# Retention and a cosine-gated MLP on one core: q is loaded four tokens to a partition, and x leaves PSUM in steps

## The chip, the cores and the metric

The kernel runs on one core of a Trainium2 chip. The metric is the device time of one execution in microseconds. Before the change it was 308.84 us, the median of three runs (305.84 to 311.0). The engines are called by the names of the profile: PE is the matrix engine (PEld its weight loads), DVE the vector engine, ACT the scalar engine, POOL GpSimd, and SP the engine that here only issues DMAs. A name with a q behind it (SPq, ACTq) is that engine's instruction queue, where DMAs are issued.

## The reference

```python
# q, k, v: (8 batches, 8 heads, 576 tokens, 64); w_in (512, 2048); w_out (2048, 512); all float32
scores = (1 / 8) * q @ k.T                       # per batch and head
Dmat   = where(i >= j, gamma[h] ** (i - j), 0)   # gamma[h] = 1 - 2 ** (-5 - h)
attn   = (scores * Dmat) @ v
x = attn.transpose(0, 2, 1, 3).reshape(4608, 512)
h = x @ w_in
out = (h * cos(h)) @ w_out                       # (4608, 512) float32
```

The decay factors into a number per query row and one per key row: gamma^(i-j) = gamma^i * gamma^(-j). So q is multiplied by gamma^i / 8 and v by gamma^(-j), a causal mask of zeros and ones is left, and what lies in earlier blocks of the sequence can be carried along as a state of 64 x 64 numbers per head.

## The kernel before

**Retention.** A batch of 576 tokens is cut into five blocks (`NCH`), four of 128 tokens and a last one of 64 (`ck_of`; `ns_of` is 2 for the long blocks and 1 for the short one). The eight heads of a block are worked on together. A block passes through these steps:

1. `load` brings k, q and v of the block from HBM in float32, each by two DMAs on SP's queue. One DMA takes four heads (`half(hs)`: heads 0 to 3 into partitions 0 to 63, heads 4 to 7 into partitions 64 to 127). A partition holds two neighbouring tokens of each of its four heads, so a row of a transfer is 2 x 64 floats, 512 bytes, in the long blocks, and 256 bytes in the short one.
2. `kcast` turns k into bfloat16, and `decay` multiplies q by the table UQ and v by the table WV, both into bfloat16. k and q land side by side in the tile KQ. These three run on POOL in most blocks, on DVE in some of the first ones.
3. k and q are transposed, so that the 64 numbers of a head lie along partitions (tile KQT). For batches 0 and 1 `turn` does that on PE, with a copy by ACT; from batch 2 on `prep_dma` has SP issue one DMA transpose per block.
4. `scores` multiplies k and q by PE, for each of the two token places of a partition and for head pairs, into the PSUM banks SC; DVE multiplies by the mask MK and leaves the tile RT.
5. `rest` adds up, in the PSUM tile PS, the part from the state and the part from RT and v, and in further columns of PS the block's share of the next state. ACT then copies the result into the bfloat16 tile XT, which holds x transposed: features along partitions, tokens along columns. Columns of PS stand in the order of the token's place in its partition first (64 tokens of place 0, then 64 of place 1); the copy reads them straight and writes every second column, so that XT is in the tokens' order. `state` adds the block's share to the running state.

The tables UQ and WV are made in `consts` at the start: POOL writes token numbers into IP (`iota`), DVE corrects them for the upper 64 partitions, and ACT takes sixteen small exponentials, one per head and table.

**The MLP.** x is worked on in nine tiles of 512 tokens. `mlp1` multiplies XT by w_in for one of sixteen groups of 128 hidden features, ACT takes the cosine, and DVE multiplies. The second product is done for the first tile by `mlp2` in the plain way, and for the others by `layer2`, with seven products of quarter size and sums of quarters in place of eight products.

**The order.** Everything is written out by hand in `emit`, and each engine runs its own instructions in that order, held back only by semaphores. PE has two things to do in turn: the MLP of tile j, and in between the blocks of batch j + 1. Within `layer2` of tile j the five blocks of batch j + 1 are visited at steps 0, 3, 6, 9 and 12 (`VISITS`: `rest` of the block before, `scores` of this one). `prep_dma` of blocks 0 and 1 of batch j + 2 stands in `layer2` of tile j (`PREP2`), that of blocks 2 to 4 in `mlp1` of tile j + 1 (`PREP1`).

**SP's queue.** At the start SP issues k, q and v of the five blocks of batch 0, in that order. After that `loads_to` keeps the loads three blocks ahead of the preparation (`LEAD`). Each of the fifteen staging tiles (k, q, v for five blocks) exists once, so a load waits until the cast or decay of the batch before has read its tile. From batch 2 on SP issues for each block a transpose, which waits for that block's three POOL instructions, and then the six loads of a later block. The stores of the result go out on ACT's queue, but for the last ones. The weights are loaded by POOL's queue in eight transfers, which cast to bfloat16, in the first 50 us.

The change touches `load`, `decay`, `scores`, `rest` and `consts`.

Of the kernel before, what the change touches and what calls it, by code (L numbers as in the profile page):

```python
# [6 lines left out]
ALU = mybir.AluOpType  # L7
# [7 lines left out]
NP = H_ // 2  # L15
# [28 lines left out]
def ns_of(r):  # L44

    return ck_of(r) // 64


# [92 lines left out]
class _Kernel:  # L141
    def __init__(self, nc, es, q, k, v, w_in, w_out, out):
# [52 lines left out]
        self.bOSB = [Buf() for _ in range(4)]  # L195
        self.IP = sb("ip", [128, NIP], F32)
        self.WV = sb("wv", [128, NIP * 4], F32)
        self.UQ = sb("uq", [128, NIP * 4], F32)
# [6 lines left out]
        self.C_PIH = sb("c_pih", [128, 1], F32)  # L205
        self.bIP, self.bWV, self.bUQ, self.bMK, self.bC, self.bID, self.bIDLE = (Buf() for _ in range(7))

# [19 lines left out]
    def consts(self):  # L227
        s = self.s
        s.op("dve", lambda e: e.memset(self.C_LN8.ap(), float(math.log(1.0 / 8.0))), writes=[Buf()])
        s.op("dve", lambda e: e.memset(self.C_PIH.ap(), float(math.pi / 2.0)), writes=[self.bC])  # L230
        s.op("dve", lambda e: e.memset(self.IDLE.ap(), 0.0), writes=[self.bIDLE])
        self.touch(AF.Exp)

        for t, b, o, n, pat, base, mul in (
                (self.IP, self.bIP, 0, NIP, [[CH, NCH - 1], [1, 2]], 0, 2),
                (self.IP, self.bIP, NIP - 1, NIP, [[0, 1]], CH * (NCH - 1), 1),
                (self.MI, self.bMK, 0, 2 * CH, [[-1, 2], [1, 2], [2, 64]], 0, -2)):
            shape = [[n, 128]] + [[1, 1]] if o else [[n, 128], [1, n - 1]] if n == NIP else [[n, 128], [128, 2], [64, 2], [1, 64]]
            s.op("pool", lambda e: e.iota(bass.AP(t, o, shape), pat, base=base, channel_multiplier=mul,
                                          allow_small_or_imprecise_dtypes=True), writes=[b])  # L240
        for o, n in ((0, NIP - 1), (NIP - 1, 1)):
            up = bass.AP(self.IP, 64 * NIP + o, [[NIP, 64], [1, n]])
            s.op("dve", lambda e: e.tensor_scalar(up, up, -128.0 if n > 1 else -64.0, None, ALU.add),
                 reads=[self.bIP], writes=[self.bIP])
# [12 lines left out]
        for t, b, sign in ((self.UQ, self.bUQ, 1.0), (self.WV, self.bWV, -1.0)):  # L257
            for h in range(H_):
                hs, hh = divmod(h, 4)
                s.op("act", lambda e: e.activation(  # L260
                    bass.AP(t, 64 * hs * 4 * NIP + hh, [[4 * NIP, 64], [4, NIP]]),
                    bass.AP(self.IP, 64 * hs * NIP, [[NIP, 64], [1, NIP]]), AF.Exp, scale=sign * self.lng[h],
                    **(dict(bias=bass.AP(self.C_LN8, 64 * hs, [[1, 64], [1, 1]])) if sign > 0 else {})),
                    reads=[self.bIP, self.bC], writes=[Buf()])
            b.w = [Tok("act", "act", s.count["act"], {})]

# [6 lines left out]
    def load(self, x, b, r, after=()):  # L273
        ns = ns_of(r)
        t, bt = self.ST32[x][r], self.bST32[x][r]

        def half(hs):
            dst = bass.AP(t, 64 * hs * 256 * ns, [[256 * ns, 64], [D_ * ns, 4], [1, D_ * ns]])
# [3 lines left out]

        return self.s.dma("sp", f"{x}n{r}", [half(0), half(1)], writes=[bt], after=after)

# [26 lines left out]
    def decay(self, eng, x, b, r):  # L311
        ns, i = ns_of(r), b % 2
        if x == "q":
            o, bt, w, bw = self.by_head(self.KQ[i][r], 256 * ns, 512 * ns, ns, D_, 256), self.bQB[i][r], self.UQ, self.bUQ
        else:
            o, bt, w, bw = self.by_head(self.VB[i][r], 0, 256 * ns, ns, D_ * ns, D_), self.bVB[i][r], self.WV, self.bWV
        self.s.op(eng, lambda e: e.tensor_tensor(  # L317
            o, self.by_head(self.ST32[x][r], 0, 256 * ns, ns, D_ * ns, D_),
            bass.AP(w, r * 8, [[4 * NIP, 128], [1, 4], [4, ns], [0, D_]]), ALU.mult),
            reads=[self.bST32[x][r], bw], writes=[bt])  # L320

# [50 lines left out]
    def scores(self, b, r):  # L372
# [3 lines left out]
        for c in range(2):  # L376
            for sl in range(ns):
                for hs in range(2):
                    for hp in range(2):
# [3 lines left out]
                            bass.AP(self.KQT[i], k0 + sl * 256, [[W, 64], [1, 64]]),  # L383
                            bass.AP(self.KQT[i], k0 + 256 * ns, [[W, 64], [256, ns], [1, 64]]),
                            dict(start=c == 0 and sl == 0, stop=c == 1 and sl == ns - 1, skip_group_check=True)))
        self.group(mms, [self.bKT[i][r], self.bQT[i][r]], self.bSC)
        for hp in range(2):
            p3 = [[512, 128], [ns * nq, 2], [1, ns * nq]]
            s.op("dve", lambda e: e.tensor_tensor(  # L389
                bass.AP(self.RT[r % 2][hp], 0, p3), bass.AP(self.SC[hp], 0, p3),  # L390
                bass.AP(self.MK, 0, [[2 * CH, 128], [0, 2], [1, ns * nq]]), ALU.mult),
                reads=[self.bSC[hp], self.bMK], writes=[self.bRT[r % 2][hp]])

    def rest(self, b, r, state=True):
# [39 lines left out]
        n0 = min(ck, XR - t0)  # L434
        for x0, po0, n in ((t0, 0, n0), (0, n0 // ns, ck - n0)):
# [412 lines left out]
```

## Time and profile before

| | |
|---|---|
| time, median of 3 runs (range) | 308.84 us (305.84 to 311.0) |
| time of the profiled execution, and its span | 309.18 us, 307.1 us |
| mean granted clock of PE over the span | 0.989 |
| matmuls | 3520, busy 292.3 us |
| loads of q: transfers, size | 64 of 128 KB and 16 of 64 KB |
| q, from issue to landing (median) | 3.4 us (128 KB), 3.0 us (64 KB) |
| SP's time to issue a load of q (least, median, most) | 595, 617, 2167 ns |
| SP's time to issue a transpose (least, median, most) | 1227, 1282, 2208 ns |
| POOL's decay of q, long block (mean) | 1101 ns |
| ACT's copy of x out of PSUM (mean) | 748 ns long, 392 ns short block |
| ACT's copy of a transpose out of PSUM, 128x512 (mean) | 595 ns |
| HBM read, written | 36.70 MB, 9.44 MB |

The span is the time from the first to the last instruction of the program on the core; the time of an execution has some two microseconds more around it. In the profile's groups, a line reads: line of the source, engine, operation, tile written <- tiles read, size, count, then the busy time in us, the mean of one instruction in ns, and the idle time of the engine ahead of them with what ended it. The page cuts the span into 40 slices of 7.7 us and gives each engine's busy share in tenths; the row DMA is the mean busy share of the 16 DMA engines. A line of a DMA queue gives packets, megabytes, and the time the packets took as a share of 16 engines over the span. The chain of waits is followed back from the last instruction, and gives what each stretch of the time was spent on.

### The profile page before, as it was taken

To read this page: it belongs to the slowest core of one execution; us is meant where nothing else is said; L and a number is where in the kernel's file an instruction comes from. 1 tells how busy PE (TensorE), PEld (TensorE's weight loads), DVE (VectorE), ACT (ScalarE), POOL (GpSimd) and SP (SyncE) were. 2 spreads that over 40 slices of the span, in tenths; PEclk is the share of its full clock that TensorE was granted. 3 is DMA by queue.
4 is the path that set the end of the run, shared out by engine and by line. 5 is a ranking of instruction groups with operands and counts; after the bars stand their busy time and mean duration, and the time that the engine had idled before them with its cause. 6 is when DMAs were issued, how large, how long until landed. Compare 5 with 4: busy or idle time off the path is not lost.

```text
span 307.1 us, 8716 instructions
## 1 busy us (share of the span) xinstructions
PE 292.3 (95%) x3520; PEld 190.6 (62%) x3520; DVE 232.3 (76%) x393; ACT 190.1 (62%) x336; POOL 115.8 (38%) x133
## 2 busy tenths in 40 slices
PE   8768997999899999999999999999999999999996
PEld 3347644553587458746874687457845874685485
DVE  3347654867986898789878986999689768937963
ACT  6647845587565766576657665865576657724730
POOL 2346271999835444533551445436341000000000
PEclk9969999999999999999999999999999999999999
DMA  4999999567986987697879799977795012003003
GB/s 137 204 203 218 215 235 235 156 162 198 235 177 184 280 129 189 169 269 161 164 180 260 160 174 170 290 168 173 191 254 97 2 50 89 2 0 130 10 0 140
DMA packets 103480, 49.60 MB, mean 162 GB/s; under 512 B 45456, under 2 KB 98960, under 8 KB 103440
## 3 DMA queue, kind: packets, MB, share of 16 engines
q1 hardware_dynamic: 94176, 35.80, 54.2%
q10 hardware_dynamic: 5040, 9.05, 8.8%
q0 software_dynamic: 4224, 4.19, 8.4%
q8 instruction: 28, 0.46, 0.6%
q14 instruction: 12, 0.10, 0.1%
HBM read 36.70 MB, written 9.44 MB: 150 GB/s over the span
## 4 chain that ended last, share of the span: by engine, by line
PE 82%; DVE 5%; ACT 4%; SPq 4%; DMA 2%; issue 1%; POOL 0%; DVEq 0%; ACTq 0%
PE mm L362 59%; PE mm L364 14%; PE ps L362 6%; SPq L281 4%; PE sc L362 3%; DMA kn<-in_k_dram 2%; ACT cb L482 2%; DVE gt L485 1%; DVE ss L542 1%; DVE rt L389 1%; ACT sb L456 1%; ACT xt L439 1%; ACT kqt L348 1%; DVE ss L485 1%; DVE s L453 0%
## 5 line engine op out<-in xcount | busy, mean ns | idle before, releaser
L362 PE MATMUL mm<-xt,win 128*128 128x512 bf16 (+5 forms) x517 | 119.0, 349 | 2.0 <-DVE gt L485 1.2
L482 ACT ACTIVATE cb<-mm,c_pih 128x512 bf16<-128x512 f32 (+3 forms) x147 | 98.7, 680 | 33.7 <-PE mm L364 30.0
L485 DVE TENSOR_TENSOR gt<-mm,cb 128x512 bf16<-128x512 f32 (+1 forms) x130 | 85.7, 678 | 11.8 <-ACT cb L482 8.2
L362 PEld LDWEIGHTS mm<-xt,win 128*128 128x128 bf16 x517 | 46.8, 99 | 49.5 <-ACT cb L482 4.0
L364 PE MATMUL mm<-xt,win 128*128 128x512 bf16 (+5 forms) x147 | 54.0, 368 | 0.0
L389 DVE TENSOR_TENSOR rt<-sc,mk 128x512 bf16<-128x512 f32 (+1 forms) x80 | 44.8, 601 | 11.4 <-PE sc L364 11.4
L308 POOL CAST kq<-kn 128x512 bf16<-128x512 f32 (+1 forms) x40 | 25.2, 629 | 66.3 <-DMA kn<-in_k_dram 66.3
L317 POOL TENSOR_TENSOR kq<-qn,uq 128x512 bf16<-128x512 f32 (+1 forms) x37 | 36.9, 997 | 20.8 <-DMA qn<-in_q_dram 19.1
L362 PE MATMUL mm<-tt,ss 128*128 128x256 bf16 x336 | 43.2, 273 | 0.0
L439 ACT ACTIVATE xt<-ps 128x512 bf16<-128x512 f32 (+1 forms) x41 | 27.0, 661 | 24.6 <-PE ps L364 18.6
L317 POOL TENSOR_TENSOR vb<-vn,wv 128x512 bf16<-128x512 f32 (+1 forms) x34 | 34.4, 1013 | 17.1 <-DMA vn<-in_v_dram 14.4
L456 ACT ACTIVATE sb<-s 64x256 bf16<-64x256 f32 x64 | 26.6, 416 | 13.3 <-DVE s L453 12.1
L362 PEld LDWEIGHTS mm<-tt,ss 128*128 128x128 bf16 x336 | 31.4, 98 | 4.8
L566 ACT ACTIVATE sn<-mm 128x512 f32<-128x512 f32 x31 | 18.5, 598 | 25.1 <-PE mm L364 24.8
L542 DVE TENSOR_TENSOR ss<-gt 128x512 bf16<-128x512 bf16 (+1 forms) x56 | 32.1, 573 | 0.9
L571 DVE TENSOR_TENSOR osb<-mm,sn 128x512 f32<-128x512 f32 x30 | 20.6, 687 | 11.6 <-PE mm L364 11.3
L362 PE MATMUL mm<-wout,gt 128*128 128x256 bf16 x217 | 28.0, 273 | 0.3 <-DVE gt L485 0.3
L362 PE MATMUL mm<-wout,ss 128*128 128x256 bf16 (+1 forms) x160 | 27.4, 305 | 0.0
L453 DVE TENSOR_TENSOR s<-ps,s 128x256 f32<-128x256 f32 x24 | 10.2, 424 | 21.3 <-ACT xt L439 19.7
L364 PEld LDWEIGHTS mm<-xt,win 128*128 128x128 bf16 x147 | 14.4, 98 | 15.9
L362 PEld LDWEIGHTS mm<-wout,gt 128*128 128x128 bf16 x217 | 20.1, 98 | 4.1 <-DVE gt L485 0.5
L362 PEld LDWEIGHTS mm<-wout,ss 128*128 128x128 bf16 x160 | 15.1, 98 | 5.2
(76 smaller groups left out, 324.6 us busy)
## 6 DMA issues: line engine op xcount, KB each, us to landing
out_dram<-osb ACTq DMA_DIRECT2D x34, 256.0 KB, 3.4
kn<-in_k_dram SPq DMA_DIRECT2D x64, 128.0 KB, 3.4
qn<-in_q_dram SPq DMA_DIRECT2D x64, 128.0 KB, 3.4
vn<-in_v_dram SPq DMA_DIRECT2D x64, 128.0 KB, 3.7
win<-in_moe_w_in_dram POOLq DMA_DIRECT2D x4, 512.0 KB, 7.4
wout<-in_moe_w_out_dram POOLq DMA_DIRECT2D x4, 512.0 KB, 11.6
kn<-in_k_dram SPq DMA_DIRECT2D x16, 64.0 KB, 3.7
qn<-in_q_dram SPq DMA_DIRECT2D x16, 64.0 KB, 3.0
```

The source lines that it names most:

```text
L308: fn = (lambda e: e.activation(o, x, AF.Copy)) if eng == "act" else (lambda e: e.tensor_copy(o, x))
L317: self.s.op(eng, lambda e: e.tensor_tensor(o, self.by_head(self.ST32[x][r], 0, 256 * ns, ns, D_ * ns, D_), bass.AP(w, r * 8, [[4 * NIP, 12 ...
L362: self.nc.tensor.matmul(o, a, b, **kw)
L364: return s.done("pe", self.nc.tensor.matmul(o, a, b, **kw), reads, writes)
L389: s.op("dve", lambda e: e.tensor_tensor(bass.AP(self.RT[r % 2][hp], 0, p3), bass.AP(self.SC[hp], 0, p3), bass.AP(self.MK, 0, [[2 * CH, 128 ...
L439: s.op("act", lambda e: e.activation(o, p, AF.Copy), reads=[self.bPS], writes=self.bXT[x0 // GR:(x0 + n) // GR])
L456: s.op("act", lambda e: e.activation(bass.AP(self.SB[r % 2], 64 * hp * 512 + 64 * hp, [[512, 64], [128, NP], [1, D_]]), bass.AP(self.S32, ...
L482: s.op("act", lambda e: e.activation(ci, mi, AF.Sin, bias=self.C_PIH.ap(), scale=1.0), reads=[bm, self.bC], writes=[bcb])
L485: s.op("dve", lambda e: e.tensor_tensor(bass.AP(gt, dt * TB + o0, [[16 * TB, 128], [TB * step, k], [1, n]]), bass.AP(m, 0, [[512, 128], [n ...
L542: self.s.op(eng, lambda e: e.tensor_tensor(oo, xx, yy, op), reads=xb + yb, writes=ob)
L566: self.s.op("act", lambda e: e.activation(self.SN[k].ap(), bank[0].ap(), AF.Copy), reads=[bank[1]], writes=[self.bSN[k]])
L571: self.s.op("dve", lambda e: e.tensor_tensor(bass.AP(self.OSB, 2 * t * DM + 256 * h, [[4 * DM, 128], [DM, 2], [1, 256]]), bass.AP(bank[0], ...
```

## The change

The loads of q, and only those, get another layout. A partition now holds four neighbouring tokens (two in the short block; `nj_of`) of two heads, where it held two tokens of four heads: partitions 32 p to 32 p + 31 belong to head pair p. The two transfers of a block take the even and the odd heads (`parity(h)`), each into all 128 partitions. A row of a transfer is 4 x 64 floats, 1024 bytes, in the long blocks, and 512 bytes in the short one. k and v stay as they were.

What follows from it: `decay` reads q straight through and writes it to the same place in KQ; `scores` and `rest` take q's columns from KQT in runs of 32, and columns of PS now stand in the order of the token's place among four; the copy to XT therefore reads PSUM with a step of 32 columns, four at a time, and writes straight. The mask and its numbers follow that order. In `consts` q has token numbers of its own (IQ, four to a partition), LG holds the logarithms of gamma by partition, and the tables are made by six exponentials over all 128 partitions, whose scale is read from LG, in place of sixteen.

```diff
+def nj_of(r):
+    return ck_of(r) // 32
...
+        for h in range(H_):
+            for o, n, hd in ((0, 32, 2), (2, 64, 4)):
+                p, i = h // hd, h % hd
+                s.op("dve", lambda e: e.memset(bass.AP(self.LG, n * p * 6 + o + i, [[6, n], [1, 1]]),
+                                               self.lng[h] if o == 0 else -self.lng[h]), writes=[Buf()])
...
+        for t, b, n, w, o, c in ((self.IQ, self.bIQ, 32, 2 * NIP, 0, 2 * NIP - 2), (self.IP, self.bIP, 64, NIP, 0, NIP - 1)):
+            for p in range(1, 128 // n):
+                for o, m, k in ((0, c, CH), (c, w - c, 64)):
+                    up = bass.AP(t, n * p * w + o, [[w, n], [1, m]])
+                    s.op("dve", lambda e: e.tensor_scalar(up, up, -float(k * p), None, ALU.add),
+                         reads=[b], writes=[Buf()])
...
     def load(self, x, b, r, after=()):
+        def parity(h):
+            n = D_ * nj_of(r)
+            dst = bass.AP(t, h * n, [[2 * n, 128], [1, n]])
+            src = bass.AP(self.src[x], ((b * H_ + h) * S_ + CH * r) * D_, [[2 * S_ * D_, 4], [n, 32], [1, n]])
+            return lambda e: e.dma_start(dst, src)
...
-        return self.s.dma("sp", f"{x}n{r}", [half(0), half(1)], writes=[bt], after=after)
+        parts = [parity(0), parity(1)] if x == "q" else [half(0), half(1)]
+        return self.s.dma("sp", f"{x}n{r}", parts, writes=[bt], after=after)
...
     def decay(self, eng, x, b, r):
         if x == "q":
+            o = bass.AP(self.KQ[i][r], 256 * ns, [[512 * ns, 128], [D_, 2], [128, nj], [1, D_]])
+            x = bass.AP(t, 0, [[256 * ns, 128], [D_ * nj, 2], [D_, nj], [1, D_]])
+            w, bw, bo = bass.AP(self.UQ, 8 * r, [[4 * NIP, 128], [1, 2], [2, nj], [0, D_]]), self.bUQ, self.bQB[i][r]
...
     def scores(self, b, r):
-                            bass.AP(self.KQT[i], k0 + 256 * ns, [[W, 64], [256, ns], [1, 64]]),
+                            bass.AP(self.KQT[i], 64 * hp * W + 1024 * r + 256 * ns + 32 * (2 * hs + c),
+                                    [[W, 64], [128, 2 * ns], [1, 32]]),
...
     def rest(self, b, r, state=True):
-                     bass.AP(self.KQT[i], 1024 * r + 256 * ns + c * 128 + 64 * hs, [[W, 128], [256, ns], [1, 64]]),
+                     bass.AP(self.KQT[i], 1024 * r + 256 * ns + 32 * (2 * hs + c), [[W, 128], [128, 2 * ns], [1, 32]]),
...
-                o = bass.AP(self.XT, x0, [[NP * XR, 128], [XR, NP], [1, ns], [ns, n // ns]])
-                p = bass.AP(self.PS, po0, [[1024, 128], [256, NP], [64, ns], [1, n // ns]])
+                o = bass.AP(self.XT, x0, [[NP * XR, 128], [XR, NP], [nj, n // nj], [1, nj]])
+                p = bass.AP(self.PS, po0, [[1024, 128], [256, NP], [1, n // nj], [32, nj]])
```

More of the change, by code (lines that the diff above doesn't have):

```diff
@@ L205, in __init__ @@
         self.C_PIH = sb("c_pih", [128, 1], F32)
-        self.bIP, self.bWV, self.bUQ, self.bMK, self.bC, self.bID, self.bIDLE = (Buf() for _ in range(7))
+        self.bIP, self.bIQ, self.bLG, self.bWV, self.bUQ = (Buf() for _ in range(5))
+        self.bMK, self.bC, self.bID, self.bIDLE = (Buf() for _ in range(4))
         def ps(name):
@@ L241, in consts @@
[L241 to L244, printed above, removed]
+        for t, b, o, dims, pat, base, mul in (
+                (self.IQ, self.bIQ, 0, [[2 * NIP, 128], [4, NCH - 1], [1, 4]], [[CH, NCH - 1], [1, 4]], 0, 4),
+                (self.IQ, self.bIQ, 2 * NIP - 2, [[2 * NIP, 128], [1, 2]], [[1, 2]], CH * (NCH - 1), 2),
+                (self.IP, self.bIP, 0, [[NIP, 128], [1, NIP - 1]], [[CH, NCH - 1], [1, 2]], 0, 2),
+                (self.IP, self.bIP, NIP - 1, [[NIP, 128], [1, 1]], [[0, 1]], CH * (NCH - 1), 1),
+                (self.MI, self.bMK, 0, [[2 * CH, 128], [128, 2], [32, 4], [1, 32]], [[-1, 2], [1, 4], [4, 32]], 0, -2)):
+            s.op("pool", lambda e: e.iota(bass.AP(t, o, dims), pat, base=base, channel_multiplier=mul,
+                                          allow_small_or_imprecise_dtypes=True), writes=[b])
@@ L256, in consts @@
             s.op("dve", lambda e: e.memset(self.SB[i].ap(), 0.0), writes=[self.bSB[i]])
-        for t, b, sign in ((self.UQ, self.bUQ, 1.0), (self.WV, self.bWV, -1.0)):
-            for h in range(H_):
-                hs, hh = divmod(h, 4)
+        for t, bt, ip, bi, o, n in ((self.UQ, self.bUQ, self.IQ, self.bIQ, 0, 2),
+                                    (self.WV, self.bWV, self.IP, self.bIP, 2, 4)):
+            for i in range(n):
                 s.op("act", lambda e: e.activation(
[L261 to L265, printed above, removed]
+                    bass.AP(t, i, [[4 * NIP, 128], [n, 4 * NIP // n]]), ip.ap(), AF.Exp,
+                    scale=bass.AP(self.LG, o + i, [[6, 128], [1, 1]]),
+                    **(dict(bias=self.C_LN8.ap()) if o == 0 else {})),
+                    reads=[bi, self.bLG, self.bC], writes=[Buf()])
+            bt.w = [Tok("act", "act", s.count["act"], {})]
     def touch(self, f):
@@ L311, in decay @@
     def decay(self, eng, x, b, r):
[L312 removed]
+        ns, nj, i = ns_of(r), nj_of(r), b % 2
+        t, bt = self.ST32[x][r], self.bST32[x][r]
         if x == "q":
[L314 to L320 removed]
+            o = bass.AP(self.KQ[i][r], 256 * ns, [[512 * ns, 128], [D_, 2], [128, nj], [1, D_]])
+            x = bass.AP(t, 0, [[256 * ns, 128], [D_ * nj, 2], [D_, nj], [1, D_]])
+            w, bw, bo = bass.AP(self.UQ, 8 * r, [[4 * NIP, 128], [1, 2], [2, nj], [0, D_]]), self.bUQ, self.bQB[i][r]
+        else:
+            o = self.by_head(self.VB[i][r], 0, 256 * ns, ns, D_ * ns, D_)
+            x = self.by_head(t, 0, 256 * ns, ns, D_ * ns, D_)
+            w, bw, bo = bass.AP(self.WV, 8 * r, [[4 * NIP, 128], [1, 4], [4, ns], [0, D_]]), self.bWV, self.bVB[i][r]
+        self.s.op(eng, lambda e: e.tensor_tensor(o, x, w, ALU.mult), reads=[bt, bw], writes=[bo])
     def kqt(self, i, r, x, n):
```

18 lines of the change are left out of this document (9 added, 9 removed).

## The prediction

> **What bounds the kernel now.** I read the page first, then the chain of waits, the busy time by windows, and the issue rows of the loads. From the page:
>
> ```profile
> PE 292.3 (95%) x3520; PEld 190.6 (62%) x3520; DVE 232.3 (76%) x393; ACT 190.1 (62%) x336; POOL 115.8 (38%) x133
> ...
> DMA  4999999567986987697879799977795012003003
> ...
> q1 hardware_dynamic: 94176, 35.80, 54.2%
> q10 hardware_dynamic: 5040, 9.05, 8.8%
> q0 software_dynamic: 4224, 4.19, 8.4%
> ...
> PE 82%; DVE 5%; ACT 4%; SPq 4%; DMA 2%; issue 1%; POOL 0%; DVEq 0%; ACTq 0%
> ```
>
> TensorE is the bound, but the DMA row is almost full for three quarters of the span and empty in the last quarter. So the transfers have little to give away while they run, and TensorE has no reserve that could make up a delay. The windows say how full:
>
> ```profile
> core 0: us, PE busy (x) PEld busy (x) DVE busy (x) ACT busy (x) POOL busy (x), PEclk, DMA share, GB/s
> 0.00:30.00 30.00, 22.91 (x283) 13.73 (x284) 14.24 (x29) 17.80 (x42) 12.49 (x23) 0.89 0.96 190
> 30.00:62.00 32.00, 29.79 (x392) 17.08 (x390) 20.41 (x31) 19.64 (x37) 16.26 (x14) 1.00 1.05 210
> 62.00:82.00 20.00, 18.02 (x179) 8.62 (x176) 15.56 (x28) 14.95 (x28) 20.00 (x20) 1.00 0.73 195
> ...
> 143.70:174.10 30.40, 30.40 (x405) 20.58 (x402) 25.64 (x45) 20.23 (x35) 13.05 (x15) 1.00 0.91 191
> 174.10:204.50 30.40, 30.35 (x400) 20.41 (x400) 25.67 (x44) 20.03 (x36) 13.21 (x16) 1.00 1.00 198
> ```
>
> The second number from the right is the DMA share. Over 0 to 82 us it is 0.96, 1.05 and 0.73; in the steady tiles (30.4 us each, TensorE busy throughout) 0.82, 0.91 and 1.00 in three neighbours. Above 1 the packets' spans overlap; the highest five-microsecond stretches show 1.20 to 1.22 (15 to 20 and 35 to 50 us). So an engine that always has work gets through 1.05 to 1.2 us of packet time per us. At the start the loads also set the end:
>
> ```profile
> 0.74 0.75 SPq L281
> ...
> 13.74 7.09 DMA kn<-in_k_dram
> ...
> 20.90 0.62 POOL kq L308
> ```
>
> That is the chain: SP issues twenty transfers one behind the other until 13.7, then the program waits 7.09 us for k of block (0,3). (I write (b,r) for batch and block.)
>
> **What the change does to q's transfers.** Each block keeps two transfers of q, with half the rows: 128 rows of 1024 B where there were 256 of 512 B (512 B for 256 B in a batch's short fifth block). A row costs, by two lines of the page: q1's packets take 54.2% of 16 x 307.1 us, 28.3 ns each at 380 B; q10's 8.8%, 85.8 ns at 1796 B. The straight line between them gives 23 ns at 256 B, 34 at 512, 54 at 1024 and 96 at 2048.
>
> The other thing is where a transfer can be cut. In the old pair of patterns both sides begin with a count of 64. All other loads and stores begin with 64 or 128 on both sides, and the page's packet counts fit 16 closing writes per transfer (q10, 35 stores: 35 x 128 rows and 35 x 16 closings make its 5040). The new pair begins with 128 partitions on one side and with 4 head pairs on the other; if the pieces are dealt by the outermost count and have to match on both sides, there are only 4 pieces. Then q runs on 4 engines and not on 16. No row of this trace shows such a transfer, so its cost is bounded from both sides:
> - 16 pieces: q of a full block costs an engine 16 x 54 ns = 0.87 us where it cost 32 x 34 = 1.08; a batch (four full blocks and the short one) 4.0 us instead of 5.1: 1 us less.
> - 4 pieces: 64 x 54 ns = 3.48 us on each of four engines; a batch 16.1 us instead of 5.1: **11.0 us more** there, and 5.1 less on the other twelve, which helps nobody, since k, v, the transposes and the stores are spread over all 16 and are only done when the slowest engine is.
>
> I take 4 pieces, since both sides' outermost count is what all rows that do get 16 have in common. The Trainium skill, "DMA: Bandwidth & Descriptors", section "Why a DMA increments its semaphore by 16 and not by 1", states the same as a rule: the number of engines is the largest one up to 16 that divides the slowest dimension of both patterns. By that rule it is 4 here, and 16 in every transfer of before; no run here shows it yet.
>
> **The sum, for four engines.** *Start.* k of (0,3) stands behind three blocks of q, 3 x 2.4 = 7.2 us more work. SP gets through q faster: a 256-row issue takes 617 ns (median), a 128-row store 378, so six issues save 1.4 us. The first wait is some 5 us longer, part of it absorbed later, where blocks wait for TensorE.
>
> *Batch 2.* It is the first whose transposes are DMAs: they stand in the same queues behind all of batch 2's loads. By then four engines have 3 x 11.0 = 33.0 us more. Before, they spent 28.8 + 33.6 + 14.6 = 77.0 us of packet time in the 82 us up to there, from about 3 us on. At a rate of 1.05, 79 us can give 83: 6 are free, and the rest is (33 - 6)/1.05 = 26 us late; at 1.2 they can give 95, and it is (33 - 18)/1.2 = 12.5 us. What covers it is almost nothing: the transpose of (2,0) is issued at 76.9, lands 4.3 us later (median), and TensorE's scores of it begin at 81.8. So TensorE comes there **12 to 26 us late**, and the 5 us from the start are within that.
>
> *Steady tiles.* A batch costs an engine 0.91 x 30.5 = 27.8 us by the three windows, 25 by the prices above; with 11.0 more 36 to 39, at 1.05 to 1.2 a period of 30 to 37 us against TensorE's 30.5. Over five batches that adds 0 to 32 us; but the slack has grown by then (transpose of (7,0) issued 217.7, landed 222, used at 236.9: 15 us), and with twelve engines half idle the packets should rather get the short times. Late at (7,0): 0 (below the 12 of batch 2, which stays) to 43. TensorE's work behind that point is what it was. I take 18 us, from the middle of batch 2's two ends, with nothing added since.
>
> *The rest.* The copy of x (31 of 748 ns, 10 of 392) writes two-element steps now and contiguous runs afterwards, but reads PSUM in fours at a step of 32. Nearest rows: the copy of kqt, contiguous both ways, 595 ns for the same tile. Below: -0.15 x 31 = -4.6 us of ScalarE time; above, no row reads in such steps; a doubling would be +23 us. I take 0: ScalarE is 62% busy and these copies hold 0.8% (2.5 us) of the chain. Only the sum of states waits on them ("DVE s L453 <- ACT xt L439", 19.7 us in total), off the end's path. Scores and q times state read q in runs of 32 columns instead of 64: two runs of 64 (scores, 221 ns) cost what one run of 128 does (rt times v, 225), so 0; a tenth more on the scores' 2.9% of the chain would be +0.9 us. The masks and the decay of q keep their sizes: 0.
>
> Constants: DVE gets 16 memsets of some 60 ns and six more subtractions of 0.24 us (L243's mean), +2.4 us, against 2.57 us that it idles before q of (0,0) at 5.83; GpSimd two iotas, +0.3, and an identity some 2.4 us later, against 2.22 of idle before its first cast at 4.65; ScalarE six exponentials for sixteen (8 x 295 + 8 x 205 ns before), some 2 us less. All of it lies beside the first loads; if that cover is a bit short, 0.5 us, and SP's chain of issues still ends later.
>
> Sum: span 307.1 + 18 = 325, with the 2.1 us that lie around it (309.18 in all) **327 us**. The profiled execution is 0.1% above the median shown, 308.84.
>
> **Rivals.**
> - *Four engines, and it shows* (forecast): 327 us, 319 to 347 by the two ends. Chance 0.78.
> - *Four engines, but hidden*: a lone 1024 B packet may cost less than the line says, and the loads run three blocks ahead, some 15 us in the late tiles. For it speaks that slack, against it the absence of any at (2,0). 310 to 314 us; chance 0.08.
> - *Sixteen engines* (not slower): the destination's 128 alone decides. Place: the chain's SP issues up to 13.7 us, 6 x 0.24 = 1.4 us, and 0.2 us a block behind them. 307 us. The point where it turns is the number of pieces n: 256 x 54/n ns is under the old 1.08 us from n = 13 up, and from n = 8 (+0.65 us a block, 3 a batch) idle DMA time takes it in. Faster by 2% would need more than the chain's whole 2% of DMA waits, or the copy's 4.6 us on the path. Chance 0.11.
> - *The copy of x turns dear*: PSUM read in steps at double time, 1.5 us a block on ScalarE; 20 us a batch stay within its 30.5, but the states (19.7 us of waits) and TensorE's next block come later: 312 to 320 even with 16 engines. Against it: nothing but the missing row. Chance 0.03.
>
> That the change doesn't do what it says would show in the packet count alone; I see no way to that.
>
> **How the numbers follow.** A measurement tells some 2% (6 us) from no change. Slower: 0.78, 0.02 of the hidden case's 0.08, and the dear copy, less a small case at the low end: 0.80. Same: 0.16, the hidden case and most of the sixteen. Faster: 0.04. The range runs from 307 (sixteen engines) to 347 (batch 2 at its dear end with twelve more in the steady tiles); beyond it I leave 0.15.
>
> **What the profile after would show.** q1 with 10,240 packets fewer (83,936), if there are 16 closings a transfer; with 4, another 160 x 12 = 1,920 fewer (82,016). q's landing, 3.4 us now, two or three us longer and in the steady tiles far longer, while the mean DMA share *falls* (engines waiting for four). POOL's waits for k, q and v (66.3, 19.1 and 14.4 us in the view of waits) grow, TensorE gets waits for DMA around 20 and 82 us and its busy share drops below 92%. The time of the last 55 us, behind the loads, stays. Wrong it would be if q's landing stays near 3 us, or if the late loads meet slack at batch 2 that I missed.

## The result, and the profile after

The changed kernel takes **334.1 us** (median of four runs, 332.5 to 337.8) against 308.15 us before, a ratio of **1.085** (95% interval 1.075 to 1.095): slower by 26 us. The profiled execution took 332.51 us, its span is 330.5 us, 23.4 more than before. A median here is over all runs of a kernel, while a ratio leaves out runs more than 1.5% above its fastest (five of ten in e8, two of four in e1 and e10), so the two can seem apart below.

The page of the changed kernel, the lines that answer to those shown of before:

```profile
PE 298.5 (90%) x3520; PEld 192.9 (58%) x3520; DVE 232.6 (70%) x415; ACT 184.3 (56%) x326; POOL 112.2 (34%) x135
...
DMA  4869959555799999999689978996999803001103
...
q1 hardware_dynamic: 82976, 35.80, 59.8%
q10 hardware_dynamic: 5040, 9.05, 8.3%
...
PE 68%; DMA 14%; SPq 6%; DVE 4%; issue 3%; ACT 3%; POOL 1%; DVEq 0%; ACTq 0%; POOLq 0%
```

TensorE is down from 95 to 90% of a longer span, and of the chain it holds 68% where it held 82; DMA has gone from 2 to 14%. The packet count is the plain one: 94,176 less 10,240 rows less 960. That is 80 transfers of q with 12 closing writes fewer each, so **each transfer of q closed 4 times, not 16**. And although there are fewer packets with the same bytes, they take more of the DMA time (59.8% of a longer span for 54.2%).

Where it is lost, by windows of the changed kernel (columns as before; the DMA share is the second from the right):

```profile
0.00:30.00 30.00, 20.98 (x240) 11.02 (x244) 12.75 (x47) 14.08 (x29) 10.48 (x22) 0.89 0.71 156
30.00:62.00 32.00, 25.16 (x348) 15.80 (x344) 16.54 (x28) 17.36 (x33) 10.04 (x14) 0.94 0.91 176
62.00:82.00 20.00, 19.18 (x202) 9.96 (x203) 13.67 (x19) 11.26 (x22) 20.00 (x16) 0.92 0.55 151
82.00:113.00 31.00, 23.59 (x311) 15.71 (x310) 18.34 (x32) 14.34 (x29) 13.75 (x17) 0.89 0.88 183
...
143.70:174.10 30.40, 29.38 (x389) 19.47 (x387) 24.28 (x43) 18.58 (x32) 12.09 (x15) 1.00 0.96 184
174.10:204.50 30.40, 29.46 (x373) 19.76 (x375) 25.43 (x44) 19.11 (x34) 12.25 (x15) 1.00 1.01 181
```

Up to 82 us the DMA share is 0.71, 0.91 and 0.55 where it was 0.96, 1.05 and 0.73: on the mean of all 16 the engines idle more, while the program waits longer. That fits a few full engines, but the trace does not say which engine carried a packet. From 82 to 113 us TensorE is busy for 23.6 of 31 us, where the kernel before had 30.7:

```profile
82.00:113.00 31.00, 30.74 (x416) 20.60 (x404) 26.30 (x46) 20.42 (x36) 14.65 (x18) 1.00 0.91 203
```

From 143.7 us on about 1 us in 30.4 is missing, tile by tile.

The view of waits, in us in total, times, and the longest:

```profile
POOL kq L349 <- DMA qn<-in_q_dram: 84.2, 32, 6.8
POOL kq L335 <- DMA kn<-in_k_dram: 42.1, 30, 4.7
...
PEld sc L391 <- DMA kqt<-kq: 11.7, 5, 6.4
PE sc L391 <- DMA kqt<-kq: 11.2, 5, 6.3
```

POOL now waits for q (84.2 us, 19.1 before), and TensorE's scores wait five times for a transpose, which they never did before. One of the five, in the timeline of the changed kernel:

```profile
140.50 1.23 SPq L361 DMA_TRANSPOSE kqt<-kq  x1
...
145.95 0.25 PE L391 MATMUL sc<-kqt 64*64 64x64 bf16 x7 [0.97 <-DMA kqt<-kq]
```

It is block (3,4), the short fifth block of batch 3. Its decays ended at 133.1; the transpose got its turn on SP's queue at 140.5, and the block's scores, which began at 145.95, had by then stood 0.97 us for it. The longest of the five waits, 6.3 us, is for block (2,0); the other four, 4.9 us together, are for the fifth blocks of batches 3 to 6. In the kernel before, the transpose and the mask of block (3,4):

```profile
122.56 1.38 SPq L332 DMA_TRANSPOSE kqt<-kq  x1
...
128.74 0.48 DVE L389 TENSOR_TENSOR rt<-sc,mk 128x128 bf16<-128x128 f32 x2
```

For a clock by stage I take, from the timelines, the start of the first mask (DVE's tile rt) of each block, and give how much later it is than in the kernel before. These numbers return for each experiment:

| kernel | (0,3) | (1,3) | (2,0) | (2,4) | (7,4) | end of span |
|---|---|---|---|---|---|---|
| changed | 3.0 | 9.8 | 15.1 | 18.0 | 23.2 | 23.4 |

So 18 us are lost by the end of batch 2's blocks, 5 more between there and the last block, and nothing behind it.

Not all of the 18 is waiting. At (2,0), whose transpose came late, it is 15.1. The 2.9 that are added by (2,4) come with a lower clock of TensorE: the granted clock (PEclk, third from the right in the windows) is 0.89 from 82 to 113 us, where it was 1.00, and a narrower window has it at 0.50 from 95.8 to 102.6 us, around the end of the 6.3 us wait for that transpose. TensorE was busy for 5.1 of these 6.8 us, which at half the clock leaves some 2.5 us of work for later. That the wait brings the half clock on is argued: e8 below, where TensorE waits for nothing longer than 1 us at that place, has no such stretch there.

### The profile page after: what moved, and what is told of

Its sections match the earlier page's. It is cut to its first block, busy times and chain, and to the rows that moved or that the text cites. A ratio compares the mean times of both kernels' runs of the same rounds, so it can differ in the third digit from the quotient of the medians.

```text
span 330.5 us, 8684 instructions
## 1 busy us (share of the span) xinstructions
PE 298.5 (90%) x3520; PEld 192.9 (58%) x3520; DVE 232.6 (70%) x415; ACT 184.3 (56%) x326; POOL 112.2 (34%) x135
## 3 DMA queue, kind: packets, MB, share of 16 engines
q1 hardware_dynamic: 82976, 35.80, 59.8%
## 4 chain that ended last, share of the span: by engine, by line
PE 68%; DMA 14%; SPq 6%; DVE 4%; issue 3%; ACT 3%; POOL 1%; DVEq 0%; ACTq 0%; POOLq 0%
PE mm L391 50%; PE mm L393 11%; DMA kqt<-kq 8%; SPq L307 4%; PE ps L391 4%; PE sc L391 2%; DMA qn<-in_q_dram 2%; DMA vn<-in_v_dram 2%; ACT cb L515 2%; DVE gt L518 2%; DMA kn<-in_k_dram 2%; SPq L301 2%; DVE kq L349 1%; POOL kq L349 1%; DVE ss L518 1%
## 5 line engine op out<-in xcount | busy, mean ns | idle before, releaser
L518 DVE TENSOR_TENSOR gt<-mm,cb 128x512 bf16<-128x512 f32 (+1 forms) x130 | 85.3, 677 | 11.1 <-ACT cb L515 8.0
L349 POOL TENSOR_TENSOR kq<-qn,uq 128x512 bf16<-128x512 f32 (+1 forms) x37 | 35.4, 956 | 84.3 <-DMA qn<-in_q_dram 84.2
L393 PE MATMUL mm<-xt,win 128*128 128x512 bf16 (+5 forms) x147 | 54.2, 369 | 0.0
L335 POOL CAST kq<-kn 128x512 bf16<-128x512 f32 (+1 forms) x40 | 23.8, 595 | 42.2 <-DMA kn<-in_k_dram 42.1
L472 ACT ACTIVATE xt<-ps 128x512 bf16<-128x512 f32 (+1 forms) x41 | 22.2, 543 | 28.6 <-PE ps L393 25.7
L575 DVE TENSOR_TENSOR ss<-gt 128x512 bf16<-128x512 bf16 (+1 forms) x56 | 33.3, 594 | 0.9
L391 PE MATMUL mm<-wout,gt 128*128 128x256 bf16 x217 | 30.2, 286 | 0.4 <-DVE gt L518 0.3
L391 PE MATMUL mm<-wout,ss 128*128 128x256 bf16 (+1 forms) x160 | 28.4, 312 | 0.0
L391 PE MATMUL sc<-kqt 64*64 64x128 bf16 (+1 forms) x536 | 15.2, 222 | 12.7 <-DMA kqt<-kq 11.2
L486 DVE TENSOR_TENSOR s<-ps,s 128x256 f32<-128x256 f32 x24 | 10.2, 424 | 21.5 <-ACT xt L472 21.1
L391 PEld LDWEIGHTS mm<-wout,gt 128*128 128x128 bf16 x217 | 21.1, 103 | 5.3 <-DVE gt L518 1.2
```

Source lines behind the costliest of these rows:

```text
L335: fn = (lambda e: e.activation(o, x, AF.Copy)) if eng == "act" else (lambda e: e.tensor_copy(o, x))
L349: self.s.op(eng, lambda e: e.tensor_tensor(o, x, w, ALU.mult), reads=[bt, bw], writes=[bo])
L391: self.nc.tensor.matmul(o, a, b, **kw)
L393: return s.done("pe", self.nc.tensor.matmul(o, a, b, **kw), reads, writes)
L472: s.op("act", lambda e: e.activation(o, p, AF.Copy), reads=[self.bPS], writes=self.bXT[x0 // GR:(x0 + n) // GR])
L518: s.op("dve", lambda e: e.tensor_tensor(bass.AP(gt, dt * TB + o0, [[16 * TB, 128], [TB * step, k], [1, n]]), bass.AP(m, 0, [[512, 128], [n ...
```

## The experiments

The theory to be tested: q on four engines is the cause. The rivals: something else in the change (rows of 1024 B, the copy of x, the runs of 32 columns, the constants), or that only part of the loss comes from the engines.

**e1_pairs16: the same layout, on 16 engines.** Everything of the change stays, but a block's q comes in four transfers, one per head pair, whose two sides both begin with 32:

```diff
-        parts = [parity(0), parity(1)] if x == "q" else [half(0), half(1)]
+        def pair(p):
+            n = D_ * nj_of(r)
+            dst = bass.AP(t, 32 * p * 2 * n, [[2 * n, 32], [n, 2], [1, n]])
+            src = bass.AP(self.src[x], ((b * H_ + 2 * p) * S_ + CH * r) * D_, [[n, 32], [S_ * D_, 2], [1, n]])
+            return lambda e: e.dma_start(dst, src)
+        parts = [pair(p) for p in range(4)] if x == "q" else [half(0), half(1)]
```

> The changed kernel with one thing undone: q keeps its new place in SBUF and its rows (1024 B, 512 B in the short block), but a block's q comes in four transfers, one per head pair, whose two sides both begin with a count of 32. Theory (four engines): the 11 us a batch on four engines go, the first wait and the waits at batch 2 with them; 305 to 309 us, not slower than the kernel before. q1 counts 85,216 packets: 94,176 less 10,240 rows, plus 80 more transfers with 16 closings each. Rival (the new layout itself, by its rows, the copy of x, the runs of 32 or the constants): nothing of that is undone, it stays at 330 to 336 us.

Measured: 327.37 us, ratio 1.047 (1.036 to 1.058), span 320.0. The packet count is the expected one, and the start is cured (the table further down: (1,3) 0.8 us *early*, (2,0) 1.6 late), but the time is neither theory's. From batch 2 on the kernel falls behind again, to 12.9 us at the end. (The profiled execution, from which the lateness is read, took 321.76 us.) Both theories were too simple. The source view of its loads of q shows what I had left out:

```profile
L313 SPq DMA_DIRECT2D qn<-in_q_dram x160: 312/429/2278, 2.2 to 246.9; - x160
...
DMA to landing us min/median/max: 1.8/2.8/10.6
```

A transfer of half the size lands in 2.8 us, quickly, but SP needs 429 ns to issue each (median) and there are two more of them a block: 1.7 us of issues for 1.2. The timeline of SP in the kernel *before* says why that matters: between 112 and 202 us, fifteen blocks, its 104 DMA instructions take 84.0 us, the gaps of some 50 ns between them 5.2, and there is one wait of 0.4. **SP's queue was full already**: a transpose of a block came every 5.94 us, while TensorE took 6.15 us a block. The new theory has two resources: the engines that carry q, and SP's queue.

**e2_two: q on two engines.** The changed kernel with the source's leading count cut from 4 to 2 (four transfers a block, 64 partitions and one head parity each).

```diff
+        def two(h, g):
+            n = D_ * nj_of(r)
+            dst = bass.AP(t, 64 * g * 2 * n + h * n, [[2 * n, 64], [1, n]])
+            src = bass.AP(self.src[x], ((b * H_ + 4 * g + h) * S_ + CH * r) * D_, [[2 * S_ * D_, 2], [n, 32], [1, n]])
+            return lambda e: e.dma_start(dst, src)
+
+        parts = [two(h, g) for h in range(2) for g in range(2)] if x == "q" else [half(0), half(1)]
```

> The changed kernel, the same rows of q in four transfers a block whose source begins with a count of 2. Theory (pieces by the outermost count both sides share, always on the same lowest engines): two engines carry all of q, 32 us of packet time a batch by 54 ns a row, with 20 us of everything else; 8 batches, the weights and the stores make 460 us, which two engines get through in 385 to 440 us, and 55 us of TensorE work stand behind the last load: 440 to 500 us. Rival (the transfers are spread over different engines, or the layout costs the time): 325 to 340 us, as the changed kernel.

Measured: 421.04 us (one run). Below the 440 that I gave as the low end, far from the rival's 340. The dose works: with 4 closings a transfer 334 us, with 2 it is 421; the packet count is 82,976 again (160 transfers with 2 closings each are as many as 80 with 4). It has as many issues as e1 and is 94 us slower, so it is the engines here and not the number of issues. That they are the same two engines each time is not in the trace; the size of the loss fits it. I had priced a row at 54 ns, from a line through the page's two queues; the packet records of 1024 B have a mean of 50 ns in e2 (56 in the changed kernel), with a median of 46 in both.

**e5_xcopy: the copy of x alone.** The kernel before, with the copy's two patterns turned round.

```diff
-                o = bass.AP(self.XT, x0, [[NP * XR, 128], [XR, NP], [1, ns], [ns, n // ns]])
-                p = bass.AP(self.PS, po0, [[1024, 128], [256, NP], [64, ns], [1, n // ns]])
+                o = bass.AP(self.XT, x0, [[NP * XR, 128], [XR, NP], [ns, n // ns], [1, ns]])
+                p = bass.AP(self.PS, po0, [[1024, 128], [256, NP], [1, n // ns], [64, ns]])
```

> The kernel before with the copy of x alone turned round: it reads PSUM in pairs at a step of 64 columns and writes XT straight. Theory (the copy's time is set by its steps on the writing side, and the copy is off the end's path): 128x512 falls from 748 to some 600 ns, and the time stays within 1% of before. Rival (reading PSUM in steps is dear and is part of the loss): the copy takes 900 ns or more and the time rises by 3 us or more.

Measured: 308.61 us, ratio 1.000 (0.996 to 1.004). Its groups:

```profile
L439 ACT ACTIVATE xt<-ps 128x512 bf16<-128x512 f32 x31 | 18.5, 597 | 21.9 <-PE ps L364 15.9 <-PE sc L364 5.1
L439 ACT ACTIVATE xt<-ps 128x256 bf16<-128x256 f32 x10 | 3.7, 377 | 3.7 <-PE ps L364 3.7
```

597 ns in place of 748, the time of a copy that is straight on both sides. Reading PSUM in steps costs nothing, writing SBUF in steps did. The changed kernel has 597 too. It takes 4.7 us of ScalarE off and no time with it: this rival is out.

**e6_split: SP's queue alone.** The kernel before, its layout, rows and 16 engines, but q in four transfers a block.

```diff
+        def two(hs, g):
+            dst = bass.AP(t, 64 * hs * 256 * ns + 2 * g * D_ * ns, [[256 * ns, 64], [D_ * ns, 2], [1, D_ * ns]])
+            src = bass.AP(self.src[x], ((b * H_ + 4 * hs + 2 * g) * S_ + CH * r) * D_,
+                          [[D_ * ns, 64], [S_ * D_, 2], [1, D_ * ns]])
+            return lambda e: e.dma_start(dst, src)
+        parts = [two(hs, g) for hs in range(2) for g in range(2)] if x == "q" else [half(0), half(1)]
...
```

> The kernel before, with a block's q in four transfers (two heads each, 64 partitions, 512 B rows, both sides begin with 64) in place of two. Same rows, same layout, all 16 engines; only SP has two issues a block more. Theory (SP's queue is full in the steady tiles, 6.01 us of its 6.1 us a block, so what it gets more goes into the time): some 0.5 us a block more, from batch 3 on late by 10 to 13 us, 316 to 322 us, the start as before. Rival (the four-transfer kernel lost its 14 us to its rows or its layout): SP's time is covered, 307 to 311 us.

Measured: 342.76 us, ratio 1.106 (1.101 to 1.112). The sign is as the theory has it, the size is not: from (2,4) to (7,4) it loses 19 us, where I expected 10 to 13, and 12.5 us are lost before, where I expected nothing. The issue row says why:

```profile
L287 SPq DMA_DIRECT2D qn<-in_q_dram x160: 595/608/1641, 2.2 to 268.2; - x160
```

I had counted on some 0.3 us for an issue of half the rows. It takes 608 ns, as long as one of twice as many: two more a block are 1.2 us and not 0.5, and SP's transposes come every 7.14 us in place of 5.94. So a kernel with nothing changed but how its loads of q are cut is slower than the changed kernel.

**e8_pool: e1 with SP relieved.** From batch 2 on, two of the four head pairs are issued by POOL's queue (the edit, against e1).

```diff
+        if x == "q" and b > 1:
+            w0, r0 = bt.w, bt.r
+            self.s.dma("sp", f"{x}n{r}", parts[:2], writes=[bt], after=after)
+            w1 = bt.w
+            bt.w, bt.r = w0, r0
+            self.s.dma("pool", f"p{x}n{r}", parts[2:], writes=[bt], after=after)
+            bt.w = w1 + bt.w
+            return bt.w[0]
```

> The kernel with q in four transfers of one head pair, but from batch 2 on two of the four are issued by POOL's queue. Theory (SP's queue is what was left of the loss): SP has 0.9 us a block less, the lateness that grew from batch 3 on goes, 306 to 313 us; POOL has two issues of some 0.8 us a block more, 1.6 of the 6 us of which it is busy 2.5. Rival (the layout or the rows): stays at 322 to 328 us.

Measured: 312.19 us, ratio 1.001 (0.996 to 1.007), span 309.1. The lateness no longer grows: 2.7 us at (2,4), 1.8 at (7,4). The new layout, its rows, its copy, its runs of 32 and its constants are all in this kernel, and it is as fast as the one before.

**e7_inter: two transfers and 16 engines.** The changed kernel with head pairs interleaved over the partitions (4 i + p for 32 p + i). The source can then begin with 32 in two transfers of 128 rows; q's columns are read at a step of 4. The tables are made to suit by some more small operations on DVE.

```diff
-            src = bass.AP(self.src[x], ((b * H_ + h) * S_ + CH * r) * D_, [[2 * S_ * D_, 4], [n, 32], [1, n]])
+            src = bass.AP(self.src[x], ((b * H_ + h) * S_ + CH * r) * D_, [[n, 32], [2 * S_ * D_, 4], [1, n]])
...
-                            bass.AP(self.KQT[i], 64 * hp * W + 1024 * r + 256 * ns + 32 * (2 * hs + c),
-                                    [[W, 64], [128, 2 * ns], [1, 32]]),
+                            bass.AP(self.KQT[i], 64 * hp * W + 1024 * r + 256 * ns + 2 * hs + c,
+                                    [[W, 64], [128, 2 * ns], [4, 32]]),
...
```

> The changed kernel with head pairs interleaved over the partitions (partition 4 i + p in place of 32 p + i): a block's q still comes in two transfers of 128 rows of 1024 B, but the source now begins with 32 and the destination with 128; q's columns are read at a step of 4 by scores and rest, and the tables are built to suit. Theory (four engines first, SP's queue second): q on 16 engines and with fewer issues; SP some 0.4 us a block below the kernel before, so neither binds: 303 to 309 us, q1 at 83,936 packets. Rival (1024 B rows, the copy of x, the constants or the order of q's columns cost the time): 315 us or more.

Measured: 321.32 us, ratio 1.038 (1.034 to 1.043). This is the rival's range, and one of the rival's four reasons, the order of q's columns; but the step of 4 that it comes from is e7's own, and not in the changed kernel. The theory's two resources are free here: the packet count is 83,936 as expected, and the loads run ahead (a transpose every 5.81 us). TensorE itself has more to do. The first line of e7's page, the busy time of each engine:

```profile
PE 305.1 (96%) x3520; PEld 197.3 (62%) x3520; DVE 237.5 (74%) x416; ACT 184.5 (58%) x326; POOL 113.3 (36%) x136
```

Two of e7's groups by form, TensorE's reads of q's columns (busy time, mean ns of one, idle time before them):

```profile
L414 PE MATMUL sc<-kqt 64*64 64x128 bf16 x480 | 20.2, 288 | 1.1 <-ACT kqt L400 1.1
...
L414 PE MATMUL ps<-kqt,sb 128*128 128x128 bf16 x96 | 15.0, 291 | 1.6 <-DVE rt L444 1.6
```

and the same two groups of the changed kernel, which reads q in runs of 32:

```profile
L391 PE MATMUL sc<-kqt 64*64 64x128 bf16 x480 | 13.2, 224 | 7.5 <-DMA kqt<-kq 6.3 <-ACT kqt L377 1.2
...
L391 PE MATMUL ps<-kqt,sb 128*128 128x128 bf16 x96 | 9.5, 223 | 1.4 <-DVE rt L421 1.4
```

Runs of 32 cost what runs of 64 did (221 and 220 ns in the kernel before); single columns at a step of 4 cost 288 and 291. TensorE is busy 305.1 us instead of 292.3, and the span is 11.9 us longer than before. It is 96% busy: this kernel is bound by TensorE again, with more work for it. The remedy for the transfers worked and was paid for elsewhere.

**e10_relief: is it SP's queue or the four engines, in the changed kernel?** There, too, SP's queue is full in the steady tiles (15 blocks in 95.8 us, waits of 0.4), since a transpose now takes 1.94 us to issue where it took 1.41 (means over those blocks). Either that is SP's own matter, or SP only stands before full engines. One of v's two transfers goes to POOL's queue from batch 2 on, written as in e8 with `x == "v"`, `parts[:1]` and `parts[1:]`.

> The changed kernel (q in two transfers with a source that begins with 4) with the second of v's two transfers issued by POOL's queue from batch 2 on. Theory (SP's queue, filled by transposes that take 1.94 us to issue in place of 1.41, sets the steady tiles): SP has 0.65 us a block less; the 8 us that are lost from batch 3 on go, the 15 us up to batch 2 stay: 322 to 327 us. Rival (the four engines themselves are full in the steady tiles): the transfers are late whoever issues them, 331 to 336 us.

Measured: 337.77 us, ratio 1.083 (1.074 to 1.091), no gain. SP issues less, and is as full as before, for its transposes take longer still (2.46 us, the mean of 15 blocks). The rows of the transposes, least/median/most in ns, first of the kernel before, then of the changed one, e10 and e2:

```profile
L332 SPq DMA_TRANSPOSE kqt<-kq x30: 1227/1282/2208, 76.9 to 232.5; - x30
```
```profile
L361 SPq DMA_TRANSPOSE kqt<-kq x30: 1227/1852/4727, 93.1 to 261.9; - x30
```
```profile
L369 SPq DMA_TRANSPOSE kqt<-kq x30: 1190/2352/5482, 90.0 to 266.0; - x30
```
```profile
L367 SPq DMA_TRANSPOSE kqt<-kq x30: 1216/2736/4871, 127.6 to 353.4; - x30
```

The least stays at 1.2 us in all; the median goes up as q's engines get fewer (1.28, 1.85 on four, 2.74 on two), and stays at 1.29 in e1, where q is on 16. The transposes do not wait for their data meanwhile: in batches 3 to 6 of the changed kernel a block's last decay had ended 5.5 us or more before its transpose began on SP. So the time SP loses goes with the loaded engines, and relieving SP of other work gives nothing back here. That SP stands still because those engines' queues are full is argued from these rows; the queues themselves do not show in the trace. And e10 is not a clean test of the time: POOL issues in its own order, which may have delayed v, and it is 16.8 us late already at (1,3), 7.0 more than the changed kernel. What it shows is that the pace behind that did not get better (6.53 us a block for 6.43).

**e3_late4 and e4b_early4: the two stages apart.** Batches 0 to 2 in the form of e1 and 3 to 7 as changed; and batches 0 to 2 as changed and 3 to 7 in the form of e8.

```diff
 # e3_late4
...
+        q = [pair(p) for p in range(4)] if b < 3 else [parity(0), parity(1)]
+        parts = q if x == "q" else [half(0), half(1)]
 # e4b_early4
...
+        parts = [pair(p) for p in range(4)] if b > 2 else [parity(0), parity(1)]
+        parts = parts if x == "q" else [half(0), half(1)]
+        if x == "q" and b > 2:
...
```

> The changed kernel with q of batches 0 to 2 in four transfers of one head pair (16 engines) and q of batches 3 to 7 as changed (a source that begins with 4). Theory (two losses: 15 us while the loads of batches 0 to 2 are behind, and some 1.6 us a batch afterwards, because a batch's work on the four engines takes longer than TensorE's 30.5 us): batch 2's scores as with four transfers throughout, 1 to 3 us late, and from batch 3 on the lateness grows by 1.6 us a batch: 316 to 321 us. Rival (the steady loss is only what is left over from a late start, which uses up the slack): 308 to 312 us.

Measured: 321.03 us, ratio 1.042 (1.039 to 1.045), at the theory's upper end. The parts fit less well than their sum: 2.7 us at (2,0), as expected, but 5.0 by (2,4), and from there 5.2 us, 1.0 a batch where I had 1.6.

> The other way round: q of batches 0 to 2 as changed, q of batches 3 to 7 in four transfers of one head pair, two of them issued by POOL (the form that took 312 us throughout). Theory: TensorE comes 15 us late to batch 2's scores and then runs at its own pace, neither gaining nor losing: 322 to 327 us. Rival (the late start is made up from the slack of the later loads): 312 to 316 us. The two runs' losses against the kernel before should add up to the 25 us of the change.

Measured: 327.27 us, ratio 1.064 (1.060 to 1.068), again at the upper end.

All kernels side by side, by their profiled executions: lateness in us against the kernel before, and the pace in us a block between (3,0) and (7,0), twenty blocks, of SP's transposes and of the masks behind TensorE's scores:

| kernel | (0,3) | (1,3) | (2,0) | (2,4) | (7,4) | end | SP | TensorE |
|---|---|---|---|---|---|---|---|---|
| before | 0 | 0 | 0 | 0 | 0 | 0 | 5.94 | 6.15 |
| changed | 3.0 | 9.8 | 15.1 | 18.0 | 23.2 | 23.4 | 6.48 | 6.43 |
| e1, 16 engines, 4 issues | -1.1 | -0.8 | 1.6 | 4.0 | 12.7 | 12.9 | 6.63 | 6.58 |
| e2, two engines | 15.6 | 30.9 | 48.8 | 56.3 | 111.9 | 112.1 | 8.80 | 8.80 |
| e5, copy of x alone | -0.9 | -1.0 | -1.1 | -1.2 | -2.3 | -2.1 | 6.05 | 6.11 |
| e6, old layout, 4 issues | 2.7 | 4.0 | 9.6 | 12.5 | 31.7 | 31.7 | 7.14 | 7.11 |
| e7, interleaved | 0.0 | 1.4 | 2.5 | 3.7 | 11.5 | 11.9 | 5.81 | 6.47 |
| e8, SP and POOL | 1.4 | 1.7 | 2.9 | 2.7 | 1.8 | 2.0 | 5.78 | 6.13 |
| e10, v half on POOL | 2.7 | 16.8 | 18.1 | 19.4 | 27.4 | 27.6 | 6.68 | 6.53 |
| e3, late four | -1.1 | 0.6 | 2.7 | 5.0 | 10.2 | 10.5 | 6.46 | 6.43 |
| e4b, early four | 5.1 | 11.1 | 16.9 | 18.7 | 17.9 | 18.1 | 5.83 | 6.13 |

The row of e5, a kernel as fast as the one before by its ratio, shows what two executions can differ by: some 2 us. Two things come out of the table. Except in e7, where its own work grew, TensorE goes at 6.11 to 6.15 us a block while SP's transposes come faster than that, and at their pace within 0.15 us when they come slower. And the change's loss comes apart by stage: the four engines in batches 0 to 2 alone cost 18.7 us by (2,4), of which 0.8 at most are won back behind it (e4b); in batches 3 to 7 alone they cost 5.2 us between (2,4) and (7,4) (e3), as much as the changed kernel loses there. The losses of the two runs add up to more than 26 us (13 and 19) mostly because e3 has one of its own: it is 5.0 us late by (2,4) from the four issues of its early batches, which e1 shows as well (4.0).

No version came out faster than the kernel before; e5 and e8 are level with it.

## Why the prediction was right

The forecast was 327 us, slower, by four engines; the time is 334.1 us, and the mechanism that sets most of the loss is the one named.

- **Four pieces.** Right, and to the packet: 4 closings a transfer. My count for that case (82,016) missed all the same, by a slip: I took 160 transfers of q for 80 (8 batches, 5 blocks, 2 each). The count for 16 closings, 83,936, was sound (e7 has it), and less 80 x 12 it is the 82,976 measured. The rule of the Trainium skill ("DMA: Bandwidth & Descriptors", section "Why a DMA increments its semaphore by 16 and not by 1") agrees with it, and with e2, where the shared count is 2 and the closings are 2.
- **The start.** "Some 5 us longer": 3.0 at (0,3). Right in kind.
- **Batch 2.** TensorE 12 to 26 us late at (2,0), 18 taken: 15.1 there. Right, and e4b shows that the four engines in batches 0 to 2 are enough for it (16.9). That the 18 which were taken equal the 18.0 at (2,4) is luck: the last 2.9 of these go with TensorE's half clock, which is no term of the sum.
- **The steady tiles.** Wrong in size, and the reason for 5.2 of the 7.1 us that the forecast is short (1.6 more is the profiled execution's distance from the median, 332.51 and 334.1). I gave a period of 30 to 37 us a batch (measured: 6.43 x 5 = 32.2), but took nothing for it, since I looked for slack at (7,0), where there are 15 us. The block that binds is the fifth one. In the kernel before the transpose of (3,4) was issued at 122.6, which with the median 4.3 us is 126.9, and its mask started at 128.7. From landing to mask the fifth blocks of batches 2 to 4 had under 2 us, those of batches 5 and 6 had 3.4 and 6.4, where (7,0) had 15. So a period of 32 us goes into the time almost at once: 5.2 us from (2,4) on.
- **SP's queue.** Not in the sum at all, beyond the "1.4 us" saved by cheaper issues. That saving is wrong: I took a store's 378 ns for 128 rows, and q's issue has a median of 573 ns in the changed kernel. And I read the loads' lateness as the DMA engines' alone, while SP took 5.94 us a block, 97% of TensorE's 6.15, and was the next thing to bind, as e6 shows with 33 us.
- **The copy of x, the runs of 32, the constants.** Each taken at nothing: right together (e8), the copy also alone (e5), where it got faster and not dearer.
- **What the profile would show.** TensorE below 92% (90), the last 55 us unchanged (55.7 and 55.9 from (7,4) to the end): right. TensorE's long wait for a DMA came too (at 91 us, for the transpose of (2,0)), and up to 82 us the DMA share fell. Not right: the DMA share did not fall in the steady tiles (0.96 and 1.01 for 0.91 and 1.00), where packets took longer: those of 256 B a mean of 43 ns from 113 to 204 us, 30 before, at the same median of 18, which I take for waiting. q's landing, by the last semaphore event of a block's two transfers, grew by the two or three us forecast (median 3.4 to 6.2), but more up to 82 us (7.7) than in the steady tiles (5.8), where I had it far longer. And of POOL's waits only that for q grew, while those for k and v fell (66.3 to 42.1, 14.4 to 8.7); the likely reason is that k and v had landed by the time that q let POOL go on.

The rival of sixteen engines was put at 307 us. Its price was right by e8 (1.001), but no kernel here has them in two issues at no other cost: four issues fill SP's queue (e1), and the interleaving that keeps two makes TensorE read in steps (e7).

## What to carry to other kernels

Before a load is given another layout, look at the leading count on both sides of its transfer: the bytes and rows can stay the same or get better and the transfer still end up on four engines of sixteen, and everything that shares those engines then goes at their pace. Count what an issuing queue does per step as one counts an engine: here SP was at 97% of TensorE's time a block without appearing as busy in any row, and two more issues a block cost more (33 us, e6) than the change itself (26). Look for slack at the tightest of the repeated steps, not at the first.

## What the hardware showed that was not expected

- The time to issue a load did not follow its rows. Medians on SP: 617 ns for 256 rows of 512 B (64 partitions, 16 engines), 608 for 128 of 512 B (64 partitions, e6), 615 for 128 of 1024 B (128 partitions, e7), 573 for 128 of 1024 B on four engines, 429 for 64 of 1024 B (32 partitions, e1); a store of 128 rows of 2048 B on ACT's queue 378. On POOL's queue the 64 rows took 552 ns (e8).
- TensorE reads its moving operand in runs of 32 columns at no cost (223 ns for 128 columns), and single columns at a step of 4 for 291 ns.
- TensorE's granted clock was 0.50 for 6.8 us around the end of a 6.3 us wait in the changed kernel, and 1.00 from there to the end of the program, with waits of up to 1.6 us.
- ScalarE's copy of 128x512 from PSUM takes 748 ns when it writes every second bfloat16, and 597 when it reads every 32nd or 64th float and writes straight.
- A transpose's issue took SP from 1.2 up to 5.5 us; its median was 1.28 us with q on 16 engines, 1.85 on four and 2.74 on two.
